# A fused attention and gated convolution kernel: from a scheduler's order to a hand-ordered four-stage pipeline

## The chip, the cores and the metric

The kernel runs on one core of a Trainium2 chip. Times are device microseconds (us) of one execution. A run counts as slow when it is over 1.5% above the fastest run of the same kernel; comparisons below use fast runs. The granted clock is TensorE's clock as the profile shows it, 1 for full speed and 0.5 for half. Engines: TensorE (PE, with its weight loads PEld), VectorE (DVE), ScalarE (ACT), GpSimd (POOL) and SyncE (SP, which here only issues DMA).

## The reference, cut to what matters

Batch B = 4, heads H = 8, sequence S = 768, head dimension D = 48; all tensors are fp32.

```python
state = zeros(B, H, D, D)
for t in range(S):                       # r, k, v: [B, H, S, D]; w, u: [H, D]
    cur = einsum('bhd,bhe->bhde', u * k[:, :, t], v[:, :, t])
    y[:, :, t] = einsum('bhd,bhde->bhe', r[:, :, t], state + cur)
    state = w * state + einsum('bhd,bhe->bhde', k[:, :, t], v[:, :, t])
x = y.transpose(0, 2, 1, 3).reshape(B, S, H * D)         # 384 channels
gate = sigmoid(sum(conv_w[i] * x shifted by 4 - i tokens, i = 0..4))   # causal
out = (gate * (x @ w_val)) @ w_out
```

A chunk of 128 tokens turns this into matrix products: scores `at` = kT x rT under a triangular mask, the state `z` carried from chunk to chunk with decay, and the bonus of `u`, which multiplies each token's own `v` by one number per head (`s`, giving `dv`). All operands of r and k are first scaled by powers of `w`.

## The kernel before, cut to what the change and the argument touch

The program is written unit by unit (a unit is two chunks, 256 tokens; there are twelve), and a scheduler orders the instructions on each engine. r, k and v come through the queue of SyncE, the weights in 32-row and 16-row pieces through the queue of ScalarE.

```python
def load(b):                                   # batch 0 is loaded by chunk instead
    for t_, src in zip(stage, (r, k, v)):      # tiles [128, H, NCH, 64], 48 of 64 used
        nc.sync.dma_start(out=...[:, :, 0:D],
                          in_=src[b].rearrange("h (c p) d -> p (h c) d", p=128))
# ... constants, then the weights:
for dst, src in ((wv_st, moe_w_val), (wo_st, moe_w_out)):
    for h in range(H):
        nc.scalar.dma_start(...)               # 32 rows
        nc.scalar.dma_start(...)               # 16 rows
# ...
for b in range(B):
    load(b)
    for cu in range(NU):
        # r scaled on GpSimd, k on VectorE, v cast on GpSimd
        for dst, src in ((rT, rs), (kT, ks)):
            tr = ps_tr.tile([128, U, NP, 128], BF16)
            # 8 transposes on TensorE: tr[:, cl, p, :] = src[:, cl, p] transposed
            nc.scalar.copy(out=dst, in_=tr)    # contiguous
        # pr = rT * kT; s = pr x u (TensorE); dv = v * s (GpSimd)
        for cl in range(U):
            # scores, mask, y = z-part + at-part + dv-part in 128x32 column tiles,
            # xT copy (ScalarE), next state, decay
        # conv -> sigmoid (ScalarE), value, product (VectorE), projection,
        # o_sb copies (ScalarE), output DMA
```

## Time and profile before

| kernel before | |
|---|---|
| median of four fast runs | 178.85 us (178.59 to 179.22) |
| the profiled run | 184.33 us, slow, span 182.4 us, mean granted clock 0.914 |
| TensorE / ScalarE / VectorE / GpSimd busy | 69 / 35 / 44 / 43% |
| transposed r copied out of PSUM | 12 copies of 1012 ns |

The prediction below reads the idle start, the waits and the unit period of this profile. Two more views carry weight later. The first is the costliest groups of instructions on its page: line, engine, operation, output and input, shapes and count; then total busy us and the mean ns of one; then the idle time ahead of them and what ended it.

```profile
L242 ACT COPY rT<-tr_ps 128x1024 bf16<-128x1024 bf16 x12 | 12.1, 1012 | 26.5 <-DMA wo_st<-in_moe_w_out_dram 19.6
L242 ACT COPY kT<-tr_ps 128x1024 bf16<-128x1024 bf16 x12 | 12.2, 1015 | 13.8 <-PE tr_ps L237 13.7
```

The table of waits (total us, times, longest):

```profile
POOL dv L260 <- DVE s_sb L258: 43.5, 10, 8.1
...
PE y_ps L311 <- POOL dv L260: 7.9, 11, 1.7
```

GpSimd makes `dv` in the same unit in which TensorE needs it, and TensorE waits for it 7.9 us in eleven places. The change moves that a whole iteration ahead.

### The profile page before, as it was taken

The numbers are of one execution on the slowest core, as the hardware profiler recorded it, in microseconds if no ns is written. First come the engines' busy times: TensorE is split into PE (matmuls) and PEld (weight loads), VectorE is DVE, ScalarE is ACT, GpSimd is POOL, SyncE is SP. The second block draws the span as 40 slices with busy tenths as digits, with TensorE's granted clock in tenths as the row PEclk, the third lists the DMA queues.
The fourth block names the chain that finished last, engine by engine and source line by source line (L and its number), as shares of the span: only waits on it lengthen the run. The fifth ranks groups of instructions, "written<-read, shape, count | busy, mean of one in ns | idle before, by whom it ended". The sixth has DMA issues, their size and how long they took to land.

```text
span 182.4 us, 4832 instructions
## 1 busy us (share of the span) xinstructions
PE 125.7 (69%) x2107; PEld 86.2 (47%) x2107; DVE 79.5 (44%) x132; ACT 63.8 (35%) x104; POOL 77.6 (43%) x107
## 2 busy tenths in 40 slices
PE   0000054219599696959999869998996989899680
PEld 0000042107376564736757447575664757575450
DVE  0121105049386754424349262564953555355220
ACT  2430002402272722613445232452644345263221
POOL 8991397023980605507229232372617142201200
PEclk9999999999859999695699965999999799999789
DMA  5999999999930695925939996951102010110202
GB/s 105 159 161 185 175 186 176 170 166 165 165 54 0 172 162 160 173 34 153 164 92 190 165 163 156 182 133 60 34 0 90 0 69 24 50 40 2 87 0 86
DMA packets 38237, 20.55 MB, mean 113 GB/s; under 512 B 20421, under 2 KB 38218, under 8 KB 38218
## 3 DMA queue, kind: packets, MB, share of 16 engines
q1 hardware_dynamic: 36096, 19.07, 58.6%
q10 hardware_dynamic: 2122, 1.19, 4.2%
q8 instruction: 16, 0.26, 0.6%
q14 instruction: 3, 0.02, 0.1%
HBM read 15.54 MB, written 4.72 MB: 111 GB/s over the span
## 4 chain that ended last, share of the span: by engine, by line
PE 43%; DMA 19%; issue 15%; POOL 12%; ACT 5%; DVE 3%; ACTq 1%; DVEq 0%; POOLq 0%
PE mm_ps L363 12%; PE y_ps L311 9%; DMA wo_st<-in_moe_w_out_dram 7%; POOL dv L260 6%; PE mm_ps L373 5%; PE mm_ps L402 5%; DMA wv_st<-in_moe_w_val_dram 5%; PE tr_ps L237 4%; DMA k_st<-in_k_dram 4%; POOL rs L215 4%; PE at_ps L273 3%; DMA wt<-in_w_dram 3%; DVE hT L395 2%; ACT gate L394 2%; PE mm_ps L249 1%
## 5 line engine op out<-in xcount | busy, mean ns | idle before, releaser
L260 POOL TENSOR_TENSOR dv<-v_st,s_sb 128x384 bf16<-128x384 f32 x24 | 20.7, 882 | 43.5 <-DVE s_sb L258 43.5
L282 DVE TENSOR_TENSOR at<-at_ps,mask 128x1024 bf16<-128x1024 f32 x24 | 29.3, 1220 | 16.6 <-PE at_ps L273 16.5
L237 PE MATMUL tr_ps<-ident,rs 128*128 128x128 bf16 x96 | 12.3, 261 | 27.3 <-POOL rs L215 25.3
L215 POOL TENSOR_TENSOR rs<-r_st,dq 128x384 bf16<-128x384 f32 x24 | 26.5, 1121 | 9.0 <-PE tr_ps L237 9.0
L363 PE MATMUL mm_ps<-xT,cwdiag 128*128 128x256 bf16 x180 | 28.0, 305 | 1.1 <-ACT xT L320 0.6
L227 POOL CAST vb<-v_st 128x384 bf16<-128x384 f32 x24 | 14.7, 616 | 24.7 <-PE y_ps L311 24.6
L363 PEld LDWEIGHTS <-cwdiag 128*128 128x128 bf16 x180 | 19.2, 108 | 7.2 <-issue 2.8
L221 DVE TENSOR_TENSOR ks<-k_st,dk 128x384 bf16<-128x384 f32 x24 | 17.3, 734 | 10.5 <-DMA k_st<-in_k_dram 7.4
L242 ACT COPY rT<-tr_ps 128x1024 bf16<-128x1024 bf16 x12 | 12.1, 1012 | 26.5 <-DMA wo_st<-in_moe_w_out_dram 19.6
L237 PEld LDWEIGHTS <-rs 128*128 128x128 bf16 x96 | 7.6, 115 | 29.3 <-POOL rs L215 26.8
L320 ACT CAST xT<-y_ps 128x384 bf16<-128x384 f32 x24 | 11.5, 481 | 22.8 <-PE y_ps L311 22.8
L242 ACT COPY kT<-tr_ps 128x1024 bf16<-128x1024 bf16 x12 | 12.2, 1015 | 13.8 <-PE tr_ps L237 13.7
L373 PE MATMUL mm_ps<-xT,wval 128*128 128x256 bf16 x108 | 16.8, 286 | 0.0
L402 PE MATMUL mm_ps<-wout,hT 128*128 128x384 bf16 x72 | 15.8, 328 | 1.5 <-DVE hT L395 0.5
L311 PE MATMUL y_ps<-ident,dv 128*32 128x128 bf16 x384 | 11.3, 247 | 7.9 <-POOL dv L260 7.9
L409 ACT COPY o_sb<-mm_ps 128x384 f32<-128x384 f32 x24 | 11.5, 479 | 13.1 <-PE mm_ps L402 13.0
L273 PE MATMUL at_ps<-rT,kT 48*128 48x128 bf16 x192 | 14.8, 246 | 0.9 <-ACT rT L242 0.6
L388 DVE TENSOR_TENSOR hT<-mm_ps,gate 128x512 bf16<-128x512 f32 x12 | 8.3, 692 | 15.9 <-PE mm_ps L373 15.7
L311 PE MATMUL y_ps<-at,vb 128*32 128x128 bf16 x384 | 13.3, 244 | 2.7 <-issue 2.0
L384 ACT ACTIVATE gate<-mm_ps 128x512 bf16<-128x512 f32 x12 | 7.2, 597 | 16.9 <-PE mm_ps L363 16.9
L237 PE MATMUL tr_ps<-ident,ks 128*128 128x128 bf16 x96 | 11.2, 254 | 1.5 <-issue 1.5
L245 DVE TENSOR_TENSOR pr<-rT,kT 128x1024 bf16<-128x1024 bf16 x12 | 9.4, 786 | 6.2 <-ACT kT L242 4.8
(57 smaller groups left out, 135.9 us busy)
## 6 DMA issues: line engine op xcount, KB each, us to landing
out_dram<-o_sb SPq DMA_DIRECT2D x12, 384.0 KB, 2.7
r_st<-in_r_dram SPq DMA_DIRECT2D x6, 192.0 KB, 4.4
k_st<-in_k_dram SPq DMA_DIRECT2D x6, 192.0 KB, 4.3
v_st<-in_v_dram SPq DMA_DIRECT2D x6, 192.0 KB, 4.5
wv_st<-in_moe_w_val_dram ACTq DMA_DIRECT2D x8, 48.0 KB, 3.8
wo_st<-in_moe_w_out_dram ACTq DMA_DIRECT2D x8, 48.0 KB, 3.7
w_bc<-in_w_dram SPq DMA_DIRECT2D x1, 192.0 KB, 3.7
wv_st<-in_moe_w_val_dram ACTq DMA_DIRECT2D x8, 24.0 KB, 4.2
```

The lines of the kernel that those rows point to most:

```text
L215: nc.gpsimd.tensor_tensor(out=rs[:, cl, :, :, 0:D].rearrange("p n two d -> p (n two) d"), in0=r_st[:, :, c, 0:D], in1=dq, op=ALU.mult,)
L221: nc.vector.tensor_tensor(out=ks[:, cl, :, :, 0:D].rearrange("p n two d -> p (n two) d"), in0=k_st[:, :, c, 0:D], in1=dk, op=ALU.mult,)
L227: nc.gpsimd.tensor_copy(heads(vb[:, cl]), v_st[:, :, c, 0:D])
L237: nc.tensor.transpose(tr[:, cl, p, :], src[:, cl, p].rearrange("p two x -> p (two x)"), ident,)
L242: nc.scalar.copy(out=dst, in_=tr)
L260: nc.gpsimd.tensor_tensor(out=heads(dv[:, cl]), in0=v_st[:, :, cu * U + cl, 0:D], in1=s_sb[:, cl, :, None].to_broadcast([128, H, D]), op=A ...
L273: nc.tensor.matmul(out=at_ps[:, par, p, :], lhsT=kT[rows, cl, p, :], rhs=rT[rows, cl, p, :], start=(p == 0), stop=(p == NP - 1), skip_grou ...
L282: nc.vector.tensor_tensor(out=at.rearrange("p a n i -> p (a n) i"), in0=at_ps.rearrange("p a n i -> p (a n) i"), in1=mask[:, None, :].to_b ...
L311: nc.tensor.matmul(out=y_ps[32 * q : 32 * q + 32, T, :], lhsT=lt, rhs=rh, start=q not in first, stop=(kind == "d" and T2 == 1), skip_group ...
L363: nc.tensor.matmul(out=o, lhsT=cwdiag[:, T, t, :], rhs=xT[:, T, t0 + t : t0 + t + W], start=(t == 0), stop=(t == KW - 1),)
L373: nc.tensor.matmul(out=o, lhsT=wval[:, kt, T, :], rhs=xT[:, kt, PAD + t0 : PAD + t0 + W], start=(kt == 0), stop=(kt == NT - 1),)
L402: nc.tensor.matmul(out=o_ps, lhsT=hT[:, T, cl * C : (cl + 1) * C], rhs=wout[:, T, :], start=(T == 0), stop=(T == NT - 1),)
```

## The change

Intent: take the order out of the scheduler's hands. A loop of 15 iterations holds four stages of different units: transposes of k (x), scores and state (a, one unit behind), y (two behind), convolution to projection (f, three behind). Matmuls of the same array shape stand together. r of a whole batch is loaded one batch ahead, six consecutive tokens of a head in one row of 1152 bytes instead of one token in 192 bytes, and scaled in groups of two of the six. All large loads and the weights go through SyncE. Cut to the core:

```diff
-    ps_y = ...bufs=1        # y had its own PSUM buffer
-    ps_mm = ...bufs=2
+    ps_mm = ...bufs=3
+    ctx.enter_context(tc.manual_schedule())
+    def load_kv(n, which): ...         # one unit of k and v, contiguous [128, U, H, D] tiles
+    def load_r(b):
+        for hh in range(2):
+            nc.sync.dma_start(out=r_st[b][:, hs, :],
+                in_=r[b, hs].rearrange("h (p j) d -> p h (j d)", j=J))     # J = 6
@@ transposes of r
-            nc.scalar.copy(out=dst, in_=tr)
+        nc.scalar.copy(
+            out=st["rT", b].rearrange("x n (p j) -> x j n p", j=J)[:, 2 * g : 2 * g + 2],
+            in_=tr)
@@ y of a unit
-            kinds = (["z"] if c > 0 else []) + ["a", "d"]       # per chunk
+        for kind, cl in (("z", 0), ("z", 1), ("a", 0), ("d", 0), ("a", 1), ("d", 1)):
@@ order
+    load_kv(1, "kv"); load_weights()                            # 25 loads on SyncE
+    for i in range(N + 3):
+        x, a, y, f = i, i - 1, i - 2, i - 3
+        if ok(x + 2): load_kv(x + 2, "kv")
+        if x % NU == 0 and x // NU + 1 < B: load_r(x // NU + 1)
+        if ok(a): prod(a)
+        if ok(x): transp_k(x)
+        if ok(f): conv(f)
+        ... scale_k(x+1); bonus, scores, state of a (first chunk); scale_r; cast_v(x+1)
+        if ok(f): value(f)
+        ... scores, state of a (second chunk)
+        if ok(y): y_out(y)
+        if b1 < B: transp_r(b1, x % NU)     # r of the next batch, b1 = x // NU + 1
+        if ok(f): project(f)
+        if i == 0: ...                      # convolution and value weights prepared
```

Partition row p of the loaded r holds tokens 6p to 6p+5, so a transpose delivers every sixth token, and the copy puts its 128 results at positions p * 6 + j of `rT`: 2-byte elements, 12 bytes apart.

## The prediction

> **What bounds the kernel now.** I read the page first (busy shares, the 40 slices), then the waits, the stretches of 2 us, and last the matmuls in order of time in the second half. Busy shares mislead here, for the span has two parts with different limits.
>
> ```profile
> PE 125.7 (69%) x2107; PEld 86.2 (47%) x2107; DVE 79.5 (44%) x132; ACT 63.8 (35%) x104; POOL 77.6 (43%) x107
> PE   0000054219599696959999869998996989899680
> PEclk9999999999859999695699965999999799999789
> DMA  5999999999930695925939996951102010110202
> ...
> PEld L237 <- POOL rs L215: 26.8, 4, 23.8
> ...
> ACT rT L242 <- DMA wo_st<-in_moe_w_out_dram: 19.6, 1, 19.6
> ```
>
> Part one: TensorE does almost nothing for about 48 us (first ten slices), while the DMA row is full. The waits name it: its first transpose comes at 23.8 us, because the scaled r comes late, and ScalarE then sits for 19.6 us behind the weight loads that it issues itself. Part two: from 57 us TensorE is 80 to 95% busy and sets the pace. Three successive units start their convolution at 152.81, 162.53 and 172.34 us, so an undisturbed unit of 256 tokens takes 9.7 to 9.8 us; twelve of them would be 117 us. How that time is made up shows in TensorE's own order of time (start, duration, what):
>
> ```profile
> 119.24 0.40 PE L311 MATMUL y_ps<-rT,z 48*32 48x128 bf16 x16
> 119.57 0.41 PE L311 MATMUL y_ps<-at,vb 128*32 128x128 bf16 x16
> 119.81 0.40 PE L311 MATMUL y_ps<-ident,dv 128*32 128x128 bf16 x16
> 120.14 0.40 PE L273 MATMUL at_ps<-rT,kT 48*128 48x128 bf16 x8
> 120.47 0.26 PE L327 MATMUL kv_ps<-z,ident 128*128 128x192 bf16 x1
> 120.80 1.26 PE L363 MATMUL mm_ps<-xT,cwdiag 128*128 128x256 bf16 x10
> 121.90 0.82 PE L373 MATMUL mm_ps<-xT,wval 128*128 128x256 bf16 x6
> ```
>
> Durations overlap, so I take start to next start. Sixteen matmuls against `at` take 0.24 us up to the next row, which has the same array shape (128 rows, 32 columns); sixteen of the same length against the identity take 0.33 us up to the next row, which has another shape (48 rows, 128 columns). The change of shape costs 0.09 us, say 0.1. The same step of 0.33 ends the `z` row and the `at_ps` row. Between 152.81 and 162.53 I count 19 such changes, because the scheduler mixes transposes, scores, state and y.
>
> A third fact is the clock:
>
> ```profile
> 80.00:82.00 2.00, 0.68 (x6) 0.34 (x6) 0.00 (x0) 0.00 (x0) 0.33 (x1) 1.00 0.00 0
> 82.00:84.00 2.00, 2.00 (x28) 1.35 (x27) 0.80 (x2) 0.96 (x2) 0.92 (x2) 0.66 0.08 24
> 84.00:86.00 2.00, 2.00 (x37) 1.29 (x38) 1.33 (x3) 0.48 (x1) 2.00 (x3) 0.50 0.84 227
> ...
> 66.00:68.00 2.00, 1.80 (x31) 0.93 (x29) 1.12 (x2) 0.38 (x1) 0.00 (x0) 1.00 1.11 162
> ...
> 158.00:160.00 2.00, 1.50 (x42) 0.93 (x44) 0.70 (x3) 0.35 (x2) 1.62 (x2) 1.00 0.52 187
> ```
>
> The columns after the stretch are TensorE, its weight loads, VectorE, ScalarE and GpSimd, then granted clock, DMA share and GB/s. After the idle stretch at 80 us the clock is half for about 6 us. Such a stretch loses about 3 us of matmul time; I see six (from 48, 72, 82, 106, 140 and 172 us). The last two lines give DMA rates: loads in runs of 192 bytes move 162 GB/s at a full share; the output alone, in rows of 1536 bytes, moves 187 GB/s at 0.52, so some 360 GB/s at a full share.
>
> [...]
>
> **The change part by part.**
>
> *Steady state on TensorE.* The instruction order of the changed kernel, per unit: k transposes, convolution, bonus | scores | state | value | scores | state | z | a, d, a, d | r transposes, projection. That is 8 changes of shape instead of 19. The pure streaming per unit, from start to next start at full clock: 15 convolutions 1.60, 9 values 0.96 (0.107 each), 6 projections 0.96 (0.16 each), 16 scores 0.46 (two rows of 0.33 less 0.1), 16 transposes 0.88 (0.055 each), 96 y matmuls 1.35 (six sixteens), bonus 0.28, 16 state products 0.48, identity 0.2. Sum 7.2 us. Before: 7.2 + 19 x 0.1 + 0.5 (the wait for `dv` seen in each unit) = 9.6, which matches 9.7. After: 7.2 + 8 x 0.1 = 8.0. The `dv` wait goes, for `dv` is now made a whole iteration before it is used.
>
> *The other engines per unit*, to see whether one takes over. VectorE: masks 2 x 1.22, scaling of k 1.1 to 1.47, product 0.79, gating 0.69 + 0.42, decay 2 x 0.35, copy 0.17: 6.3 to 6.7. GpSimd: `dv` 2 x 0.88, one r scaling of double size 2.2, v casts 2 x 0.62: 5.2. ScalarE: 2 x 1.01 + 0.60 + 0.38 + 4 x 0.48 = 4.9. All are below 8.0, and the depth of four stages puts their results ahead of need. The nearest meeting is on GpSimd: r scaled by about 6.4 us into an iteration, its transposes wanted at about 6.3.
>
> *DMA per unit*: k and v 786 KB in 192-byte runs at 165 GB/s, 4.8 us; r 393 KB in runs of 1152 bytes, at an estimated 300 GB/s, 1.3 us; output 393 KB at 360, 1.1. Sum 7.2 us, just under 8.0. Before, r at 165 GB/s would have made it 8.3. So the six-token rows keep DMA from becoming the bound.
>
> *Start.* In order on one queue: w, k0, r of batch 0, v0, kv1, 25 small weight loads, kv2, r of batch 1. TensorE's in-order stream has the first transposes of batch 1 in iteration 0, and the convolution weights' transposes behind them. In 192-byte runs 2.36 MB at 165 are 14.3 us, r twice 2.36 MB at 300 are 7.9, w and the weights about 9 (bound by issues of some 0.37 us), 1.5 at the beginning and 1.5 to land: r of batch 1 is there at about 34 to 35 us. Scaling on GpSimd 2.2, transposes 0.5: 38. Then VectorE's chain of iteration 1: cwT, three diagonals 2.4, product 0.8, k scaling 1.4, copy, two masks 2.4, two decays: iteration 1 ends at about 47, iteration 2, of the same VectorE chain, at 53.
>
> *Iterations 3 to 11.* Nine full ones at 8.0 are 72, less 0.6 for each of the last three that have no r transposes: 70. Two additions. r of batch 3 is asked for in iteration 6 and used in iteration 6; its load queues behind the output and kv8 and lands about 12.5 us into it, scaled at 14.7, wanted at 6.3: a stall of about 8. Batch 2's load is issued in iteration 2 already, for no output is ahead of it: 0 to 2. And the thin iterations 1 and 2 and that stall each leave a half-clock stretch: 2 x 2.5 = 5. So iteration 11 ends at 53 + 70 + 8 + 1 + 5 = 137.
>
> *End.* Iteration 12 about 7, iteration 13 (convolution, value, y, projection) 5.3, iteration 14 (convolution to projection, a chain of waits) 4.6: 154. From the last copy (178.6) to the end of the span (182.4) it was 3.8 before; the same after: 158. The profiled run was timed at 184.33 us with a span of 182.4, so 2 more: 160. But that profiled run was 5.4 us slower than the median of the timed runs, with its half-clock stretches; part of my five for clock and my waits will be milder in fast runs, so I take 157.
>
> **Rivals.** One: the in-order queues turn into the bound. For it: r is loaded and used in the same iteration, SyncE issues loads behind outputs that wait for the projection, and DMA has only 10% to spare. If each of the iterations 3 and 6 stalls 8 us and the rest run at 9, the time is 170 to 175. Two: DMA sustains more than I think[...], and batch 1's r is in at 28 us; with a stall of 3 instead of 8, the time is 143 to 148. Three: VectorE at 6.7[...] meets the masks' double use of a single score buffer and paces the loop at 9: 165. Against it: between the two scores of a unit lie state and value, 1.5 us, and the mask takes 1.22. Four: nothing gained, because the scheduler's order was already dense. Against: it idles 48 us at the start and changes shape 19 times.
>
> **Range and chances.** The parts that I trust are the steady state (117 to about 96 us for twelve units) and an earlier start (first dense work at 53 instead of 57). The stalls and clock together are 14 us of guess, and DMA rates move the start by some 5 either way. Predicted 157 us, 8 in 10 within 146 to 169. Faster by over 2% (below 175.4) 0.96, within 2% 0.03, slower 0.01.
>
> **What would show it.** Right: successive convolution starts 8.0 to 8.3 us apart in iterations 4, 5, 9 to 11; TensorE's wait for scaled r at about 36 to 38 us as the longest of its waits, a second of 5 to 9 us around 90 us, both ended by GpSimd behind a DMA of r; half clock only after these. No wait for `dv`. Wrong: unit periods still above 9 us in undisturbed stretches (then the changes of shape weren't what cost); TensorE waiting on VectorE masks in each unit; or k loads as the releaser in most iterations (DMA bound).

The forecast's sum came to 158 us for the span and 160 timed, taken as 157. Three of its figures are estimates, and the trace before has this beside them. For the 300 GB/s of rows of 1152 bytes: 162 with runs of 192 bytes, and the extrapolated 360 with rows of 1536. For the 1.5 us at the beginning: the first DMA traffic comes at 1.5 to 2 us. For the 1.5 to land: an output takes 2.7 us from issue to landing, of which its 393 KB at 360 GB/s would be 1.1. Of the six half-clock stretches that the prediction counts, three last some 6.5 us (from 48, 82 and 106 us) and three some 3.3, so its loss of about 3 us holds for the longer three.

## The result, and the profile after

| | before | after |
|---|---|---|
| median, fast runs | 178.85 us | 168.45 us (167.62 to 169.99, four runs) |
| ratio | | 0.943 (0.936 to 0.950) |
| profiled run | 184.33 us, slow | 167.62 us, fast, span 165.8 us |
| ScalarE busy | 63.8 us | 92.9 us |
| mean of one rT copy | 1012 ns | 3620 ns |

Ratios here and below are from runs of both kernels in the same rounds, so they are not quite the ratio of the medians quoted.

The time lies at the upper end of the predicted range (146 to 169), and the gain is 10.4 us where the predicted 157.0 stood for 21.9. The page of the kernel after, busy us and then 40 slices of the span with the busy share in tenths (PEclk is the granted clock in tenths):

```profile
PE 103.5 (62%) x2123; PEld 81.6 (49%) x2123; DVE 77.2 (47%) x135; ACT 92.9 (56%) x109; POOL 58.9 (35%) x85
PE   0123100023579689596969108996969999999980
PEclk9999999999999978999999855899999999999999
DMA  4998338993187600390927940281927702020222
```

TensorE is busy for 22 us less than in the profile of the kernel before (103.5 against 125.7), as fewer changes of shape (8 a unit instead of 19) and fewer half-clock stretches (two instead of six) would have it, though part of that belongs to the slow profile. There is one break in the middle (the 23rd and 24th slice, with the clock at half towards its end and behind it), where the prediction has its stall for the r of batch 3. But ScalarE is busy for 29 us more, and the row of costliest groups says why:

```profile
L263 ACT COPY rT<-tr_ps 128x1024 bf16<-128x1024 bf16 x12 | 42.7, 3620 | 29.2 <-PE tr_ps L260 29.0
L290 ACT COPY kT<-tr_ps 128x1024 bf16<-128x1024 bf16 x12 | 12.7, 1060 | 0.0
```

Same engine, same shape, same source memory, same count as before, and the first now takes 3.6 times as long, while its twin for k, whose output is contiguous in runs of 128, is unchanged. The table of waits of the kernel after shows what is expected and what is new:

```profile
POOL rs L246 <- DMA r_st<-in_r_dram: 31.3, 4, 19.6
PE tr_ps L260 <- POOL rs L246: 28.9, 4, 19.0
PE mm_ps L448 <- ACT o_sb L495: 7.4, 5, 1.5
PE mm_ps L468 <- ACT gate L455: 3.8, 7, 2.1
```

The first two are the predicted chain: TensorE waits for scaled r, GpSimd for the DMA of r, 19 us in the start and 8.4 us before 100 us. The wait for `dv` no longer appears among TensorE's. The last two were not predicted: TensorE waits for ScalarE, 11.2 us in twelve places. One such place in order of time (start, duration, engine and what, and in brackets the idle time ahead of it with its releaser; a duration can overlap the next start):

```profile
120.57 3.58 ACT L263 COPY rT<-tr_ps 128x1024 bf16<-128x1024 bf16 x1
...
121.79 1.26 PE L448 MATMUL mm_ps<-xT,cwdiag 128*128 128x256 bf16 x10
123.77 1.07 ACT L495 COPY o_sb<-mm_ps 128x384 f32<-128x384 f32 x2
124.52 0.71 PE L448 MATMUL mm_ps<-xT,cwdiag 128*128 128x256 bf16 x5 [1.47 <-ACT o_sb L495]
...
124.73 1.03 ACT L290 COPY kT<-tr_ps 128x1024 bf16<-128x1024 bf16 x1
...
125.63 0.90 ACT L455 ACTIVATE gate<-mm_ps 128x512 bf16<-128x512 f32 x2
...
126.31 0.49 PE L468 MATMUL mm_ps<-xT,wvA 128*128 128x256 bf16 x3 [0.25 <-ACT gate L455]
```

The rT copy starts at 120.57 and holds ScalarE for 3.6 us. The copies of the projection stand behind it in ScalarE's fixed order, and they are what frees the PSUM buffers that the third convolution tile needs. TensorE stops for 1.47 us after ten of fifteen convolution matmuls, and for another 0.25 before the value matmuls. Together that is 1.7 us in this unit.

The starts of the convolution give the unit periods. In the kernel after they are, from iteration 3: 54.09, 65.17, 74.87, 84.35, 103.93, 112.31, 121.79, 130.74, 138.03, 144.68 us. So three undisturbed units behind a slow copy take 9.5 to 9.7 us (predicted 8.0), two more 8.4 and 9.0, and the first without it (130.74 to 138.03) 7.3 us, as predicted (8.0 - 0.6 = 7.4).

### The profile page after: what moved, and what is told of

Same layout as the page of the kernel before. It is cut to its first block, busy times and chain, and to the rows that moved or that the text cites. A ratio compares the mean times of both kernels' runs of the same rounds, so it can differ in the third digit from the quotient of the medians.

```text
span 165.8 us, 4872 instructions
## 1 busy us (share of the span) xinstructions
PE 103.5 (62%) x2123; PEld 81.6 (49%) x2123; DVE 77.2 (47%) x135; ACT 92.9 (56%) x109; POOL 58.9 (35%) x85
## 2 busy tenths in 40 slices
DMA packets 58863, 20.57 MB, mean 124 GB/s; under 512 B 50773, under 2 KB 58842, under 8 KB 58842
## 4 chain that ended last, share of the span: by engine, by line
PE 44%; SPq 17%; ACT 10%; issue 9%; DMA 7%; POOL 5%; DVE 5%; DVEq 0%; ACTq 0%; POOLq 0%
PE mm_ps L427 11%; SPq L73 7%; DMA r_st<-in_r_dram 7%; PE mm_ps L448 7%; PE mm_ps L488 7%; PE mm_ps L468 6%; ACT o_sb L495 4%; PE tr_ps L260 4%; SPq L192 4%; ACT kT L290 4%; PE at_ps L334 3%; POOL rs L246 3%; PE tr_ps L287 3%; SPq L81 3%; SPq L185 2%
## 5 line engine op out<-in xcount | busy, mean ns | idle before, releaser
L263 ACT COPY rT<-tr_ps 128x1024 bf16<-128x1024 bf16 x12 | 42.7, 3620 | 29.2 <-PE tr_ps L260 29.0
L246 POOL TENSOR_TENSOR rs<-r_st,dr 128x768 bf16<-128x768 f32 x10 | 18.9, 1889 | 31.3 <-DMA r_st<-in_r_dram 31.3
L438 ACT CAST xT<-mm_ps 128x384 bf16<-128x384 f32 x24 | 11.2, 479 | 32.8 <-PE mm_ps L427 32.8
L448 PE MATMUL mm_ps<-xT,cwdiag 128*128 128x256 bf16 x180 | 22.8, 274 | 7.4 <-ACT o_sb L495 7.4
L448 PEld LDWEIGHTS <-cwdiag 128*128 128x128 bf16 x180 | 17.3, 98 | 10.7 <-issue 8.2
L476 DVE TENSOR_TENSOR hT<-mm_ps,gate 128x512 bf16<-128x512 f32 (+1 forms) x24 | 12.2, 552 | 9.7 <-PE mm_ps L468 9.7
L269 DVE TENSOR_TENSOR ks<-k_st,dk 128x768 bf16<-128x768 f32 x12 | 12.0, 1002 | 1.2 <-DMA k_st<-in_k_dram 1.2
L468 PE MATMUL mm_ps<-xT,wvA 128*128 128x256 bf16 x72 | 9.8, 272 | 3.8 <-ACT gate L455 3.8
L455 ACT ACTIVATE gate<-mm_ps 128x512 bf16<-128x512 f32 (+1 forms) x24 | 10.8, 507 | 2.0 <-PE mm_ps L448 1.9
L287 PEld LDWEIGHTS <-ks 128*128 128x128 bf16 x96 | 7.6, 114 | 8.7 <-DVE ks L269 7.5
L334 PE MATMUL at_ps<-rT,kT 48*128 48x128 bf16 x192 | 10.4, 232 | 2.0 <-DVE at L346 1.9
L427 PE MATMUL mm_ps<-at,vb 128*32 128x128 bf16 x384 | 10.6, 235 | 0.0
```

The lines of the kernel that those rows point to most:

```text
L246: eng.tensor_tensor(out=rs[:, :, :, :, 0:D].rearrange("p j n a d -> p j (n a) d"), in0=r_st[b].rearrange("p h (j d) -> p j h d", d=D)[:, 2 ...
L263: nc.scalar.copy(out=st["rT", b].rearrange("x n (p j) -> x j n p", j=J)[:, 2 * g : 2 * g + 2], in_=tr,)
L287: nc.tensor.transpose(tr[:, cl, p, :], ks[:, cl, p].rearrange("p a x -> p (a x)"), ident)
L427: nc.tensor.matmul(out=ys[cl][32 * q : 32 * q + 32, T, :], lhsT=lt, rhs=rh, start=(cl, q) not in first, stop=(kind == "d" and T2 == 1), sk ...
L448: nc.tensor.matmul(out=g_ps[:, i, :], lhsT=cwdiag[:, T, t, :], rhs=xT[:, T, t0 + t : t0 + t + W], start=(t == 0), stop=(t == KW - 1),)
L468: nc.tensor.matmul(out=v_ps[:, i, :], lhsT=wvA[:, kt, T, :] if T < 2 else wvB[:, kt, :], rhs=xT[:, kt, t0 : t0 + W], start=(kt == 0), stop ...
```

## The experiments

The theory (A in the expectations): the scattered write makes the copy slow, and because it stands in front of the projection's and the gate's copies on ScalarE it holds up TensorE by about 2 us in each unit that has it. Its rivals: the copy is slow but off the path, and the period of 9.5 us comes from elsewhere (the changes of shape or VectorE); ScalarE alone is slow at such writes, so another engine would cure it; only the place of the copy in the order is bad. For the start and for the stall at 100 us, the theory is that each is a load issued late, behind others on SyncE, which issues in the written order (in the trace after, the 25 small weight loads from 12.70 to 24.72 us, 0.48 us each, and r of batch 1 only at 27.66); the rival is that DMA is simply at its limit.

The first four kernels shared one chip. Its kernel before has a median of 182.29 us, but three of its seven runs count as slow (the fast ones: 180.19 to 182.29), and the record calls these four kernels' ratios to it unclear or gives none. The other eight shared another chip, so that their medians may be set beside each other. Expectations are quoted.

### Contiguous copy, wrong result

The tokens land in the wrong places, so the result is wrong; shapes, counts and order are unchanged.

```diff
-            out=st["rT", b].rearrange("x n (p j) -> x j n p", j=J)[:, 2 * g : 2 * g + 2],
+            out=st["rT", b].rearrange("x n (j p) -> x j n p", j=J)[:, 2 * g : 2 * g + 2],
```

> ScalarE's copy of the transposed r writes a contiguous run instead of elements 12 bytes apart; the result is wrong on purpose, everything else is as in the changed kernel. Theory A (the scattered write is the lost time): the copy falls from 3.6 to about 1.0 us, convolution starts in the units that still transpose r go from 9.5 to 8.0-8.2 us apart, and the six such units give back about 9 us: 157 to 161 us. Rival B (the PSUM ring and the chain of evacuations pace the loop whatever that copy takes): the copy falls but the units stay at 9.3 us or more and the time above 166. Rival C (the shortfall lies in the two waits for r): no change above 2 us either.

Measured: 156.31 us (155.84 to 156.93), ratio 0.863 (0.855 to 0.870). Its row among the groups:

```profile
L263 ACT COPY rT<-tr_ps 128x1024 bf16<-128x1024 bf16 x12 | 12.0, 1013 | 40.5 <-PE tr_ps L260 40.3
```

The write pattern alone is worth 12.1 us against the 168.45 of the kernel after, which was timed in other rounds; with both on the second chip (below, with the copy in pairs) it is 10.9 us, from 166.12 to 155.26. Four of the units that still transpose r are now 7.67 to 7.74 us apart. From the first of them to that of iteration 10 it is 64.38 us (55.68 to 120.06) against 76.65 us after: 12.3 us, spread over seven units at 0.6 to 2.8 each, and close to the 11.2 us of waits on ScalarE. Neither the wait for `o_sb` nor that for the gate is left among TensorE's. (The first convolution comes 1.6 us later here, so the two profiled runs differ by 10.7 us.) So the copy was on the path, and the theory holds; the predicted 157 fits a kernel whose copy takes 1.01 us.

### The same tokens, written two at a time

The two tokens of a group are neighbours in `rT`. Swapping the order of the loop within the copy writes 4 bytes, then skips 8; the result is correct.

```diff
-            out=st["rT", b].rearrange("x n (p j) -> x j n p", j=J)[:, 2 * g : 2 * g + 2],
-            in_=tr,
+            out=st["rT", b].rearrange("x n (p j) -> x n p j", j=J)[:, :, :, 2 * g : 2 * g + 2],
+            in_=tr.rearrange("x j n p -> x n p j"),
```

> Same copy, correct result, but walked so that the two elements of a group that are neighbours in the target are written one after the other: runs of 4 bytes, 12 bytes apart, read scattered from PSUM instead. Theory A in the form 'each jump to another place in SBUF costs': half the jumps, so 1.9 to 2.4 us a copy and 160 to 164 us in all. If the cost goes by elements whose step isn't 1, or the scattered read of PSUM costs as much: 3.5 us or more, and 168 us or more.

Measured: 156.21 us (155.53 to 156.81), ratio 0.861 (0.851 to 0.870), correct.

```profile
L263 ACT COPY rT<-tr_ps 128x1024 bf16<-128x1024 bf16 x12 | 12.5, 1050 | 39.5 <-PE tr_ps L260 39.4
```

The expectation of 1.9 to 2.4 us and 160 to 164 us in all missed: pairs take hardly longer than contiguous elements (1013 ns), though the copy now reads PSUM in strides. It is the whole cure, and correct. The same stretch in order of time on TensorE (start, duration) has no break between convolution and value:

```profile
119.93 1.81 PE L448 MATMUL mm_ps<-xT,cwdiag 128*128 128x256 bf16 x15
121.57 0.34 PE L307 MATMUL mm_ps<-uw,pr 128*128 128x2 bf16 x8
...
122.41 0.83 PE L468 MATMUL mm_ps<-xT,wvA 128*128 128x256 bf16 x6
```

From the convolution's start to the value's it is 2.48 us here and 4.52 us in the kernel after.

### The scattered copy on VectorE

```diff
-        nc.scalar.copy(
+        nc.vector.tensor_copy(
```

> The same scattered copy on VectorE instead of ScalarE. If the cost lies in SBUF: 3 us or more on VectorE, which then has over 9 us of work a unit, and 172 to 180 us. If the cost is ScalarE's own: 1.1 to 1.3 us, VectorE 7.5 us a unit, and 157 to 162 us.

Measured: 170.92 us (170.13 to 171.63), ratio 0.943 (0.934 to 0.951). The copy takes 3597 ns, as on ScalarE, and the kernel is as slow as the kernel after (0.943 too), just under the 172 to 180 us expected. Its waits of TensorE name the new place:

```profile
PE mm_ps L307 <- DVE pr L300: 13.0, 8, 3.3
```

The product `pr` stands behind the long copy on VectorE now, and TensorE waits 13.0 us for it (2.8 in the kernel after), where it waited 11.2 us for ScalarE. So the cost is not ScalarE's own.

### The r transposes behind the projection

```diff
-        if b1 < B:
-            transp_r(b1, x % NU)
         if ok(f):
             project(f)
+        if b1 < B:
+            transp_r(b1, x % NU)
```

> Order alone: r transposes and their copy after the projection and its two copies. Theory A: ScalarE has 7.6 us of work in a unit of 9.5, so it is not full; what hurts is that the long copy stands in front of copies that TensorE waits for. Behind the projection it stands in front of the copy of k and the gate instead, so the wait of the convolution for o_sb (1.47 us in each such unit) goes and the wait of the value matmuls for the gate grows to 2 us or more: 166 to 172 us. Rival B (ring): the ring wait moves nowhere, 168 us.

Measured: 171.62 us median, 166.4 to 174.37; three of four runs, the profiled one too, were slow, so its size is inconclusive. The trace still shows where the wait goes (waits of TensorE):

```profile
PE mm_ps L468 <- ACT gate L455: 14.9, 7, 2.2
```

The wait for `o_sb` has left the list, and that for the gate has grown from 3.8 to 14.9 us: the long copy now stands in front of the gate instead. This is a slow profile, so I take from it the kind of the wait and not its size. The one fast run, 166.4 us, is no evidence of a gain over 168.45.

### The kernel after on the second chip

An unchanged copy of the kernel after, as the foot of the ladder that follows.

> The changed kernel unaltered, as the measure for the others on this chip: 0.943 of the kernel before, within its interval of 0.936 to 0.950.

Measured: 166.12 us (166.09 to 167.68). The kernel before spread from 176.07 to 183.84 us in the same rounds, with all but one of its runs counted slow, so no ratio is given (by the medians it would be 0.92). The expected 0.943 is neither met nor refuted.

### r asked for two iterations earlier

On top of the pairs: the loads of r of batches 2 and 3 are issued in iterations 1 and 4 instead of 3 and 6.

```diff
-        if x % NU == 0 and x // NU + 1 < B:
-            load_r(x // NU + 1)
+        if x == 0:
+            load_r(1)
+        if x % NU == 1 and x // NU + 2 < B:
+            load_r(x // NU + 2)
```

> With the copy in pairs (0.861 of before); r of batches 2 and 3 is loaded two iterations earlier (in iterations 1 and 4 instead of 3 and 6). Theory A: the wait of the r transposes in iteration 6 (about 9 us) is a load asked for too late; it goes, with its half-clock stretch, and nothing else changes: 9 to 11 us less, 0.80 to 0.81 of before, and convolution starts 7.7 us apart from iteration 3 to 8 without a break. Rival D (DMA is at its limit there and the load lands no earlier): the wait stays above 5 us.

What it must remove is this stretch of the kernel after (columns: stretch, then TensorE, its weight loads, VectorE, ScalarE, GpSimd, granted clock, DMA share and GB/s):

```profile
92.00:94.00 2.00, 0.00 (x0) 0.00 (x0) 1.41 (x2) 0.49 (x2) 0.00 (x0) 1.00 1.06 190
94.00:96.00 2.00, 0.00 (x0) 0.00 (x0) 0.00 (x0) 0.00 (x0) 0.00 (x0) 0.58 1.02 348
96.00:98.00 2.00, 0.00 (x0) 0.00 (x0) 0.00 (x0) 0.00 (x0) 0.00 (x0) 0.50 0.54 190
...
102.00:104.00 2.00, 2.00 (x13) 1.38 (x12) 0.00 (x0) 2.00 (x1) 0.00 (x0) 0.50 0.00 0
```

TensorE idles while r arrives at 348 GB/s, and then runs some 4 us at half clock (0.50 at 100 to 104 us). Measured: 146.68 us (145.62 to 147.55). The pairs alone take 155.26 us on this chip, so it is 8.6 us, a little under the 9 to 11 expected. The convolution starts run on without a break (86.28, 94.02, 101.69 us) and the mean granted clock is 1.0. The stall was a late request and not a limit of DMA.

### An earlier start

On top of the hoist: r of batch 1 ahead of the weights in the queue, and the preparation of the convolution weights, which stands in TensorE's order behind the r transposes, one iteration later.

```diff
     load_kv(1, "kv")
+    load_r(1)
     load_weights()
...
-        if i == 0:
+        if i == 1:
             prep_conv()
...
+        if i == 2:
             nc.scalar.copy(out=wout, in_=wo_st)
```

> As the one with hoisted loads, and r of batch 1 is loaded ahead of the weights; the preparation of the weights stands after iterations 1 and 2 instead of 0. Theory A: the 22 us wait for r of batch 1 is the queue's order (25 small weight loads in front, one issue each 0.46 us); r is there at about 20 us, dense work begins at 38 to 42 instead of 55.9, and 14 to 18 us go: 0.71 to 0.74 of before. Rival E: the weights now come later and take the wait's place (convolution of unit 0 waits for them): 4 to 8 us go, 0.76 to 0.79.

Measured: 140.28 us (139.77 to 141.25), 6.4 us below the hoist; the first convolution starts at 49.07 us instead of 54.51. The size is the rival's, the place is not: the convolution does not wait for the weights. The wait has moved to the next load behind the 25 small weight loads, k of unit 2 (waits of VectorE):

```profile
DVE ks L269 <- DMA k_st<-in_k_dram: 16.5, 2, 15.6
```

### The z and at matmuls of y not grouped

On top of the pairs alone, y is made in the order z, a, z, a, d per chunk. It is the same work with 57 more changes of array shape between the first and the last convolution.

```diff
-        for kind, cl in (("z", 0), ("z", 1), ("a", 0), ("d", 0), ("a", 1), ("d", 1)):
+        for kind, cl, T2s in (
+            ("z", 0, (0,)), ("a", 0, (0,)), ("z", 0, (1,)), ("a", 0, (1,)), ("d", 0, (0, 1)),
+            ("z", 1, (0,)), ("a", 1, (0,)), ("z", 1, (1,)), ("a", 1, (1,)), ("d", 1, (0, 1)),
+        ):
```

> With the copy in pairs (0.861 of before); the y matmuls in the order z, a, z, a, d for each half instead of z, z, a, d, a, d: the same matmuls, 6 more changes of array shape in a unit. Theory: each costs 0.09 us and TensorE sets the pace, so units are 8.2 us apart instead of 7.7 and the whole 5 to 7 us longer: 0.885 to 0.90 of before. Rival F (changes of shape are free where weights are loaded ahead): 7.7 us, 0.86.

Measured: 160.39 us (160.30 to 160.87), against 155.26 for the pairs on this chip: 5.1 us, or 0.09 us a change. By the traces it is less: from the first to the last convolution 94.79 us, against 90.97 for the pairs on this chip, so 3.8 us, or 0.07 us a change. TensorE in order of time (start, duration):

```profile
77.76 0.30 PE L430 MATMUL mm_ps<-at,vb 128*32 128x128 bf16 x8
77.98 0.30 PE L430 MATMUL mm_ps<-rT,z 48*32 48x128 bf16 x8
78.21 0.30 PE L430 MATMUL mm_ps<-at,vb 128*32 128x128 bf16 x8
78.33 0.40 PE L430 MATMUL mm_ps<-ident,dv 128*32 128x128 bf16 x16
```

Eight matmuls take 0.22 us to the next row where the shape changes, and 0.12 us from the last `at` row to the `dv` row, which has the same shape. The term of the prediction (0.1 a change) has the right size.

### The pairs again

The pairs without another edit, in the rounds of the two kernels that follow. The three kernels above are set beside it on one chip. They were run at other times.

> The changed kernel with the copy in pairs, again, as the measure for the others on this chip: 155 to 158 us.

Measured: 155.26 us (155.00 to 156.70), ratio 0.854 (0.850 to 0.859). The cure repeats on a second chip.

### Loads in the order of use

Pairs and hoist; `conv_w`, r of batch 1 and k, v of units 2 and 3 ahead of the 24 other weight loads; each weight prepared just before its use.

```diff
     load_kv(1, "kv")
+    nc.sync.dma_start(out=cw5, in_=moe_conv_w)
+    load_r(1)
+    load_kv(2, "kv")
+    load_kv(3, "kv")
     load_weights()
...
-        if ok(x + 2):
+        if x > 1 and ok(x + 2):
             load_kv(x + 2, "kv")
...
+        if f == 0:
+            nc.scalar.copy(out=wout, in_=wo_st)
```

> As 'start' (140.3 us), but k and v of units 2 and 3 are loaded ahead of the 24 weight loads, and the weights are prepared just before their first use. In 'start' the 21 us wait for r of batch 1 was replaced by a 15.6 us wait for k of unit 2, which stood behind the weights. Theory A (order of the queue): no wait above 5 us is left at the start but the one for the first loads; dense work begins at 36 to 41 us instead of 49 and the whole is 127 to 133 us. Rival E (the weights now hold the first value and projection): dense work begins as early, but a wait of 4 to 8 us for wv or wo follows, 134 to 138 us.

Measured: 138.68 us (137.33 to 139.94, of which the last counts as slow), ratio 0.764 (0.760 to 0.768). The first convolution starts at 38.86 us, inside what was expected, but the second only at 54.84: k of unit 4 now stands behind the weights and r of batch 2 in the queue, VectorE waits 7.7 us for it, and the clock falls to half at 46 to 52 us. The total missed the 127 to 133 us that was hoped for. The rival's wait for the weights is there too but small (2.2 us before the first projection). It is the second time that the wait moved to another load behind the small weight loads.

### r loaded by unit

Pairs without hoist or reorder, but r treated like k: loaded with each unit in runs of 192 bytes, scaled by one table for 128 tokens, transposed and copied contiguously.

```diff
-        for nm, src, d in (("k", k, k_st), ("v", v, v_st)):
+        for nm, src, d in (("r", r, r_st), ("k", k, k_st), ("v", v, v_st)):
...
-    load_r(0)
+    load_kv(0, "r")
...
-            load_kv(x + 2, "kv")
-        if x % NU == 0 and x // NU + 1 < B:
-            load_r(x // NU + 1)
+            load_kv(x + 2, "rkv")
...
-            out=st["rT", b].rearrange(...)[:, 2 * g : 2 * g + 2], in_=tr
+            out=st["rT", n].rearrange("x n (c i) -> x c n i", c=U), in_=tr
```

> Undoes one part of the change on top of the copy in pairs: r is loaded unit by unit in runs of 192 bytes like k, scaled and transposed one unit ahead, and its copy is contiguous. If the rows of six tokens are needed to keep DMA from binding (the prediction's reason for them: 8.3 us of DMA a unit in runs of 192 bytes): units above 8.2 us apart, 150 to 158 us. If DMA is faster than the prediction took (216 GB/s in the changed kernel's loads of k and v): 1.18 MB at 216 is 5.5, the output 1.1, 6.6 us a unit, so the pace stays at 7.7; and both waits for a whole batch of r are gone: dense work begins at 40 to 44, 132 to 138 us.

Measured: 136.45 us (135.50 to 137.41), ratio 0.750 (0.745 to 0.754), correct: the fastest of all. It has 79,599 DMA packets instead of 58,863, and DMA does not bind: the convolutions run from 43.49 us on without a break and mostly 7.7 us apart. One stretch of two us in that part:

```profile
72.00:74.00 2.00, 1.93 (x78) 1.60 (x76) 1.62 (x2) 1.17 (x3) 2.00 (x3) 1.00 1.17 234
```

TensorE is full while loads of 192-byte runs move 234 GB/s. So the six-token rows are not needed: they buy DMA share that nothing lacks, and cost a scattered copy, a large load that must be in before its batch can begin, and the order of the queue. This run changes the size, the time and the order of the loads of r at once, so it does not tell what each is worth.

### The copies by themselves

The pairs with extra copies of 1024 elements at the end, three of each kind, one kind a line: one look at the durations, no time to compare (221.27 us, state unknown).

```diff
+    scr = persist.tile([128, 8192], BF16, name="scr")
+    s32 = scr.bitcast(F32)
+    nc.scalar.copy(out=scr[:, 0:6144].rearrange("x (a b) -> x a b", b=6)[:, 0:1024, 0], in_=srcb)
+    ...   # other steps, fp32, pairs, and the same on VectorE
```

> The disputed cost by itself: after the last unit, copies of 1024 bf16 elements from SBUF to SBUF, three each, ScalarE: contiguous; bf16 at steps of 4, 8, 12, 16 bytes; fp32 at steps of 12 and 16 bytes; pairs of bf16 at steps of 12 and 32 bytes; VectorE: contiguous, bf16 at 12 bytes, fp32 at 12 bytes. [...] If it is the write of half a 4-byte word: slow at every step for bf16 (3.5 us), fast for fp32 and for pairs. The result stays right.

The instructions of seven of these lines, with minimum, median and maximum ns. On ScalarE: L577 contiguous, L581 step 8 bytes, L583 step 12, L585 step 16, L589 fp32 at step 16, L596 pairs of bf16 at step 32; on VectorE: L603 step 12.

```profile
L577 ACT COPY scr<-rT x3: 1044/1044/1047, 151.4 to 153.5; 128x1024 bf16<-128x1024 bf16 x3
...
L581 ACT COPY scr<-rT x3: 2456/2456/2457, 158.7 to 163.7; 128x1024 bf16<-128x1024 bf16 x3
...
L583 ACT COPY scr<-rT x3: 3586/3587/3587, 166.2 to 173.4; 128x1024 bf16<-128x1024 bf16 x3
...
L585 ACT COPY scr<-rT x3: 4713/4713/4714, 177.0 to 186.5; 128x1024 bf16<-128x1024 bf16 x3
...
L589 ACT CAST scr<-rT x3: 1987/1987/1987, 196.0 to 200.0; 128x1024 f32<-128x1024 bf16 x3
...
L596 ACT COPY scr<-rT x3: 1109/1110/1111, 205.3 to 207.6; 128x1024 bf16<-128x1024 bf16 x3
...
L603 DVE COPY scr<-rT x3: 1866/1866/1868, 210.1 to 213.9; 128x1024 bf16<-128x1024 bf16 x3
```

The other medians: bf16 at step 4 bytes 1327 ns, fp32 at step 12 1542, pairs at step 12 1065; on VectorE contiguous 427 and fp32 at step 12 846. The 3587 ns at 12 bytes is close to the 3620 of the kernel. The pattern that was expected did not come: bf16 at 4 bytes takes 1.33 us and not 3.5. Nor is fp32 at 12 and 16 bytes (1.54 and 1.99 us) as slow as bf16 (3.59 and 4.71). For single bf16 elements the time grows by 1.13 us for each 4 bytes of step beyond the first (1327, 2456, 3587, 4713), and fp32 or a pair of bf16 at the same or a larger step costs far less, so it is neither the step alone nor the number of separate places. What it is, the runs do not settle. Nor do they say why VectorE took 3.6 us from PSUM inside the kernel and 1.87 us here from SBUF.

## Why the prediction was wrong

**The failed step** is the line on the other engines, "ScalarE: 2 x 1.01 + 0.60 + 0.38 + 4 x 0.48 = 4.9". The first term was taken from the row of the kernel before, whose output is contiguous. The diff shows another output pattern, of which the prediction says nothing. The rT copy took 3.62 us, so ScalarE needs some 7.7 us a unit (3.62 + 1.06 for kT, 2 x 0.48, 0.61 + 0.40, 2 x 0.54). That is below the 8.0 of TensorE, and here the second half of the step failed: "All are below 8.0, and the depth of four stages puts their results ahead of need". The depth protects what is used an iteration later. The copies of the projection and of the gate are used within a microsecond or two, and stand behind the long copy in a fixed order. Hence 1.7 us of waits in the unit shown, and 1.5 to 2.0 us on five of the seven periods. Put in place, 157 + 12.3 gives 169.3 against 168.45 measured; taken out, the kernel takes 156.3.

That 157 and 156.3 agree so closely is partly luck. In the profile with the contiguous copy, iterations 3 to 11 take 78.3 us (55.68 to 134.00), where the prediction had 70 + 8 + 1 + 5 = 84; their first convolution starts 2.7 us after its 53; and from 134.00 to the end it is 22.9 us (the run was timed at 156.93), where the prediction had 23 and then took 3 off.

The other steps, by the prediction's own list:

- **Changes of shape**, 0.1 us each and 8 instead of 19 a unit: right. Without the slow copy the unit takes 7.7 us (predicted 8.0), without r transposes 7.3 (7.4), and putting changes back costs 0.07 to 0.09 us each.
- **The wait for `dv`**: gone, as predicted.
- **The start**: r of batch 1 was scaled from 34.43 us (34 to 35 predicted), and iteration 2 ended at about 53.6 (53). But it was no earlier than before: the first convolution starts at 54.09 us, and at 51.79 in the (slow) profile before. There TensorE was not quite as idle as the prediction reads it: 11.3 us of work fall into its first 48 us, the tenth slice is a 9.
- **The stall for r of batch 3**: 8.4 us (about 8), ended by GpSimd behind the DMA of r, at 100 us instead of about 90, as the slow units had pushed it back. Batch 2 did not stall.
- **Half clock**: in two stretches, 60 to 64 and 94 to 105 us, within the allowance. **The tail**: 3.5 us (3.8).
- **DMA rates**: k and v moved at 214 GB/s (DMA share 1.13), not 165, in 28 to 30 us of the trace after, where runs of 192 bytes had moved 162 (1.11) before. Their tiles are contiguous now (rows at a pitch of 256 bytes before), and each load covers a chunk, where those measured before covered a batch; whether either is the reason is not shown. r moved at 311 in the next two us (300 taken). Harmless, but the argument that rows of six tokens keep DMA from binding rested on the 165, and r by unit shows it wrong.
- **GpSimd and VectorE scaling**: 1.8 us (2.2) and 1.0 us (1.1 to 1.47); too small to matter. So is a slip in the sum for TensorE: six sixteens of 0.24 us are 1.44 and not 1.35.

Of the rivals none came true: the queue of r stalled once and not twice, a DMA faster than taken did not make the time 143 to 148, the masks did not pace the loop (TensorE waited 1.9 us for them in all). The sign of failure that the prediction named, periods above 9 us in undisturbed stretches, did appear, but the cause that it gave for it (the changes of shape weren't what cost) was not the one.

What it left on the table, on the second chip: 166.1 us as it is, 155.3 with the copy mended, 146.7 with r asked for in time, 140.3 with the earlier start, 138.7 with loads in order of use; or 136.5 with r simply loaded by unit.

## What to carry to other kernels

A row of costliest groups gives engine, shape and type, not the layout (the same shapes stood here for 1012 and 3620 ns): when a diff rearranges an output, its duration must not be carried over. A pair of neighbouring 2-byte elements written together cost hardly more than contiguous ones here (1050 against 1013 ns). An engine with spare time in its sum (ScalarE, 7.7 of 9.5 us) still set the pace here, because one copy of 3.6 us stood in its order in front of copies of 0.5 us that TensorE wanted at once (1.7 us of waits in the unit shown). And when a load is late, look at what is ahead of it in the queue before changing its form: the wait moved twice here, from one load to another behind the same small transfers (15.6 us for k of unit 2, then 7.7 us for k of unit 4).
